# Windowed attention and a Mish MLP on one core: one third of the second product's matmuls cut into two halves of 256 columns

## The chip, the cores and the metric

The kernel runs on one core of a Trainium2 chip. The metric is the device time of one execution in microseconds: 959.55 us is the median of three runs of the kernel before (958.15 to 961.64).

## The reference

Eight batches of eight heads, 576 positions, head size 64. Each query sees itself and the 127 positions before it, with a bias that falls linearly with distance; softmax; product with V. The result, 4608 tokens of 512 values, goes through an MLP without biases:

```python
h = x @ w_in                                   # 4608x512 @ 512x2048
sp = np.where(h > 20.0, h, np.log1p(np.exp(np.minimum(h, 20.0))))
g = h * np.tanh(sp)                            # Mish
return (g @ w_out).astype(np.float32)          # 4608x2048 @ 2048x512
```

## The kernel before, in words

The tokens are cut into nine chunks of 512: the first 512 positions of each batch, and a last chunk made of the 64 left over from each. Chunk 0 is computed alone; the others go in pairs (1,2), (3,4), (5,6), (7,8).

**Numbers in two parts.** The MLP's matmuls take operands of type float32r (written `f32` in the profile's shapes, as float32 is). To keep precision every operand is held as a high part and a low part, and a product is the sum of three: high by high, high by low, low by high. For the weights W_out these parts are the tiles `so` (`w_part("o", j, 0 or 1, f)`, L180). For the Mish values ScalarE writes the high part `gh` (`parts_hi`, L433) and GpSimd subtracts to get the low part `gl` (`parts_lo`, L440); both lie in one tile `gs`, of which there are three buffers shared with others.

**The first product** of a pair of chunks (tiles `m`, `product`, L687) uses seven block products instead of eight, with weight tiles `st` streamed from DRAM. Chunk 0's is `first` (L415, tile `h`).

**The second product** is `second` (L474). One call does one chunk, one half of it (256 tokens), one of eight groups `j` of 256 hidden values, and one tile `t` of 128 tokens. It issues six matmuls into the PSUM tile `po0` or `po1`, which all accumulate over the eight `j`. In each, the stationary operand is 128x128 of the Mish values and the moving one 128x512 of W_out: two with `gh` and the high part of W_out (f = 0, 1), two with `gh` and the low part, two with `gl` and the high part. There are 9 chunks x 2 halves x 8 groups x 2 tiles = 288 calls and 1728 matmuls, each preceded by a load of its own stationary operand. `store` (L487) copies a finished `po` out on VectorE or ScalarE and sends it to DRAM.

**Attention** of the next pair runs between the calls of the second product. Its matmuls have float32 operands (tiles `s`, `o`, `pt_0l` to `pt_3l`), shorter moving operands, and come in bursts; `idle` (L131) issues bf16 matmuls of a zero tile `busy` early on, 49 in all, up to seven in a row.

**What sets the order.** All work is a list of closures with due times (`put`, L730), sorted, and issued in that order; each engine's stream keeps program order (`InOrder`, L20, from whose L30 every instruction is recorded, so the profile is read by tile names). In the last stretch (from 868 us) only the second product of the last pair is left.

Of the kernel before, what the change touches and what calls it, by code (L numbers as in the profile page):

```python
# [16 lines left out]
P = 128  # L17
# [20 lines left out]
def attention_mish_mlp(  # L38
# [19 lines left out]
    NT, DM = out.shape  # L58
    S = NT // B
    DFF = w_in.shape[0] * 256  # L60
    w_ = {"i": w_in, "o": w_out}
# [3 lines left out]
    NJ = DFF // 256  # L65
# [11 lines left out]
    pe, dve, act, pool, sp = [  # L77
        InOrder(tc, e) for e in (nc.tensor, nc.vector, nc.scalar, nc.gpsimd, nc.sync)
    ]
# [100 lines left out]
    def w_part(kind, j, part, c):  # L180
        assert (kind, j) in ready
        n = 256 if kind == "i" else DM
        return wt[(kind, j)][:, part, c * n : c * n + n]
# [264 lines left out]
    po = {}  # L448
# [25 lines left out]
    def second(c, half, j, t):  # L474
        gh, gl, _ = gs[(c, half, j)]
        if j == 0:
            po[t] = ps.tile([P, DM], F32, tag=f"po{t}", name=f"po{c}_{half}_{t}")
        k = 0
        for g, w_ in ((gh, 0), (gh, 1), (gl, 0)):
            for f in range(2):  # L480
                k += 1
                pe.matmul(
                    po[t], lhsT=g[:, f, t * P : (t + 1) * P], rhs=w_part("o", j, w_, f),
                    start=(j == 0 and k == 1), stop=(j == NJ - 1 and k == 6),
                )

    def store(c, half, t):  # L487
        ob = out_tile(c, half, t)
# [45 lines left out]
    for j in range(NJ):  # L534
        t = X0 + SLOT * j
# [189 lines left out]
    for s in range(len(PAIRS) + 1):  # L725
# [7 lines left out]
        for o, c in enumerate(chunks):  # L733
            o *= 4 * NJ
            for m in range(2 * NJ):
                for t in range(2):
                    put(o + 2 * m + t, second, c, *divmod(m, NJ), t)
                    if m % NJ == NJ - 1:
                        put(o + 2 * m + t, store, c, m // NJ, t)
                if s == 0 and m >= 2:  # L740
                    t = PARTS[m - 2]
                    put(t, parts_hi, c, *divmod(m, NJ))
                    put({3.7: 4.05, 8.9: 9.05, 19.7: 20.05}.get(t, t), parts_lo, c, *divmod(m, NJ))
                elif o + m >= 2:
                    put(o + 2 * m - 4.1, parts, c, *divmod(m, NJ))
# [11 lines left out]
        if s < len(PAIRS):  # L757
# [30 lines left out]
            for k in range(len(PROD)):  # L788
                n = 1 if s == 0 and k < 2 else 2
                for i in range(0, NF // 2, n):  # L790
# [4 lines left out]
                    for m in range((1, 2, 1, 2, 2, 3, 2)[k]):  # L795
                        t = L + 8 * k + i + n + (0, 0.6, 2.5)[m] * (1 if m else 0)
                        if s == 0 and k < 2:
                            t = (t - 0.4, L + 24.6 + 0.8 * i)[m]
                        if m == 1 and k in (3, 5):
                            t = L + 8 * k + i + n + 0.1  # L800
# [90 lines left out]
```

## Time and profile before

| | |
|---|---|
| median of three runs | 959.55 us |
| the profiled execution | 960.24 us |
| its span (first to last instruction) | 958.5 us |
| mean granted TensorE clock | 0.996 |
| TensorE matmul busy | 936.0 us (98%) |
| TensorE weight load busy | 750.6 us (78%) |
| VectorE, ScalarE, GpSimd busy | 485.2, 416.3, 374.9 us |

A matmul's recorded time contains a pipeline that overlaps the next matmul's, so its mean of 395 ns is not what it costs. The cost of one is the pitch, the distance from one start to the next, which comes out of a run's length divided by its count. PEld rows are the weight loads, which are recorded beside the matmuls.

### The profile page before, as it was taken

How to read it: one execution, taken by the hardware profiler on the slowest of the kernel's cores; microseconds unless marked ns; L12 is line 12 of the kernel's file. 1: busy time of each engine (PE TensorE's matmuls, PEld its weight loads, DVE VectorE, ACT ScalarE, POOL GpSimd, SP SyncE). 2: the span in 40 equal slices, each digit the busy share in tenths (PEclk: the TensorE clock that was granted, in tenths of full speed). 3: DMA queues.
4: the chain of work that ended last, by engine and by line, in shares of the span. 5: the costliest groups of instructions: out<-in, count | busy, mean ns of one | idle time of the engine just before them, and what ended most of it. 6: DMA issues, size and time to landing. Idle time of an engine off the chain costs nothing.

```text
span 958.5 us, 14123 instructions
## 1 busy us (share of the span) xinstructions
PE 936.0 (98%) x5133; PEld 750.6 (78%) x5137; DVE 485.2 (51%) x1280; ACT 416.3 (43%) x978; POOL 374.9 (39%) x292
## 2 busy tenths in 40 slices
PE   8998899998999999999999999999999999999998
PEld 4676677776888888888888888888888888888886
DVE  6888876684545554554555645455455105451000
ACT  5784654544455343352453534343634224243221
POOL 3201777523443434104544343014534430344443
PEclk9999999999999999999999999999999999999999
DMA  9999335787403233565221324555120144540010
GB/s 371 427 420 422 114 110 185 265 303 249 168 29 108 62 88 110 168 203 192 88 71 65 108 66 142 201 185 197 41 68 15 68 154 156 200 150 0 23 34 34
DMA packets 53286, 145.24 MB, mean 152 GB/s; under 512 B 9056, under 2 KB 10464, under 8 KB 49888
## 3 DMA queue, kind: packets, MB, share of 16 engines
q1 hardware_dynamic: 51840, 143.54, 42.6%
q8 instruction: 41, 0.67, 0.3%
q10 hardware_dynamic: 1376, 0.79, 0.3%
q14 instruction: 29, 0.24, 0.1%
HBM read 113.90 MB, written 30.41 MB: 151 GB/s over the span
## 4 chain that ended last, share of the span: by engine, by line
PE 82%; DVE 1%; DMA 1%; ACT 1%; POOL 0%; issue 0%; POOLq 0%
PE po L30 39%; PE m L30 30%; PE s L30 7%; PE o L30 5%; DMA st<-wcS 1%; PE pt_3l L30 1%; PE pt_2l L30 1%; PE pt_1l L30 1%; PE pt_0l L30 1%; ACT pz L30 0%; DVE pz L30 0%; DVE B L30 0%; POOL pz L30 0%; ACT cw L30 0%; DVE xT L30 0%
## 5 line engine op out<-in xcount | busy, mean ns | idle before, releaser
L30 PE MATMUL po<-so,gs 128*128 128x512 f32 x1728 | 411.7, 395 | 0.0
L30 PEld LDWEIGHTS po<-so,gs 128*128 128x128 f32 x1728 | 321.1, 189 | 65.8
L30 PE MATMUL m<-xT,st 128*128 128x512 f32 x768 | 177.8, 392 | 2.8 <-DMA st<-wcS 2.8
L30 PEld LDWEIGHTS m<-xT,st 128*128 128x128 f32 x768 | 145.1, 189 | 34.3 <-ACT x L30 2.3
L30 PE MATMUL m<-x,st 128*128 128x512 f32 x576 | 135.5, 392 | 1.0 <-DVE B L30 0.8
L30 POOL TENSOR_TENSOR pz<-pz,sm 128x512 f32<-128x512 f32 x64 | 66.6, 1042 | 165.9 <-DVE sm L30 67.0
L30 PEld LDWEIGHTS m<-x,st 128*128 128x128 f32 x576 | 107.1, 188 | 24.5 <-DVE B L30 0.9
L30 ACT ACTIVATE pz<-pz,mx 128x128 f32<-128x128 f32 x256 | 99.4, 390 | 43.0 <-DVE mx L30 40.6
L30 POOL TENSOR_TENSOR D<-A,C 128x1024 f32<-128x1024 f32 x16 | 38.3, 2395 | 162.7 <-DVE A L30 133.3
L30 DVE COPY ob<-po 128x512 f32<-128x512 f32 (+1 forms) x19 | 12.9, 678 | 154.3 <-PE po L30 153.2
L30 DVE TENSOR_TENSOR pz<-s,masks 128x1024 f32<-128x1024 f32 x56 | 66.3, 1216 | 35.5 <-PE s L30 32.6
L30 PE MATMUL s<-qk 64*128 64x256 f32 (+1 forms) x512 | 58.6, 365 | 3.5 <-ACT g L30 3.4
L30 DVE CUSTOM_DVE_ANT_0 pz<-s,nb 128x128 f32<-128x128 f32 x256 | 59.2, 287 | 2.8
L30 DVE TENSOR_TENSOR A<-m,A 128x1024 f32<-128x1024 f32 x32 | 39.2, 1224 | 40.3 <-PE m L30 40.3
L30 POOL TENSOR_TENSOR gs<-D,gs 128x512 fp32r<-128x512 f32 x32 | 41.1, 1288 | 43.0 <-ACT gs L30 43.0
L30 POOL TENSOR_TENSOR C<-A,C 128x1024 f32<-128x1024 f32 x16 | 38.4, 2400 | 48.7 <-DVE A L30 37.2
L30 POOL TENSOR_TENSOR gs<-B,gs 128x512 fp32r<-128x512 f32 x32 | 41.0, 1285 | 33.6 <-ACT gs L30 33.4
L30 POOL TENSOR_TENSOR gs<-A,gs 128x512 fp32r<-128x512 f32 x32 | 41.1, 1288 | 32.0 <-ACT gs L30 31.8
L30 PEld LDWEIGHTS s<-qk 64*128 64x128 f32 x512 | 41.1, 187 | 12.1 <-ACT g L30 3.8
L30 POOL TENSOR_TENSOR gs<-C,gs 128x512 fp32r<-128x512 f32 x32 | 40.9, 1286 | 23.0 <-ACT gs L30 23.0
L30 PE MATMUL o<-pz,va 128*64 128x128 f32 (+1 forms) x560 | 48.7, 320 | 0.0
L30 DVE COPY_PREDICATED s<-older,s 128x256 f32<-128x256 uint16 x64 | 35.8, 559 | 24.7 <-PE s L30 24.7
(155 smaller groups left out, 1051.4 us busy)
## 6 DMA issues: line engine op xcount, KB each, us to landing
st<-wcS SPq DMA_DIRECT2D x64, 512.0 KB, 4.6
st<-wr SPq DMA_DIRECT2D x48, 512.0 KB, 5.5
qk<-in_qk_dram SPq DMA_DIRECT2D x31, 640.0 KB, 4.9
va<-in_v_dram SPq DMA_DIRECT2D x28, 320.0 KB, 3.3
wi<-in_moe_w_in_dram SPq DMA_DIRECT2D x8, 1024.0 KB, 14.5
wo<-in_moe_w_out_dram SPq DMA_DIRECT2D x8, 1024.0 KB, 19.7
wr<-si SPq DMA_DIRECT2D x8, 1024.0 KB, 13.1
wcS<-cw SPq DMA_DIRECT2D x16, 512.0 KB, 5.8
```

The lines of the kernel that those rows point to most:

```text
L30: ins = method(*args, **kwargs)
```

## The change

In `second` the two matmuls with `gl` (the fifth and sixth of a call, `k > 4`) are each issued as two, over columns 0 to 255 and 256 to 511 of W_out and of `po`, with the same stationary operand. The other four are as before. Every matmul of the call gets `skip_group_check=True`, an argument of the program's builder, not of the instruction. No load, wait, buffer or due time is changed.

```diff
         for g, w_ in ((gh, 0), (gh, 1), (gl, 0)):
             for f in range(2):
                 k += 1
-                pe.matmul(
-                    po[t], lhsT=g[:, f, t * P : (t + 1) * P], rhs=w_part("o", j, w_, f),
-                    start=(j == 0 and k == 1), stop=(j == NJ - 1 and k == 6),
-                )
+                for d in range(2 if k > 4 else 1):
+                    n = slice(256 * d, 256 * d + 256) if k > 4 else slice(0, DM)
+                    pe.matmul(
+                        po[t][:, n], lhsT=g[:, f, t * P : (t + 1) * P], rhs=w_part("o", j, w_, f)[:, n],
+                        start=(j == 0 and k == 1), stop=(j == NJ - 1 and k == 6), skip_group_check=True,
+                    )
```

## Rows read from the trace of the kernel before

**Rows 1.** The page, its head and parts 1 and 4: busy time of the engines, and the chain of waits by engine and by line (share of the span).

```profile
span 958.5 us, 14123 instructions
PE 936.0 (98%) x5133; PEld 750.6 (78%) x5137; DVE 485.2 (51%) x1280; ACT 416.3 (43%) x978; POOL 374.9 (39%) x292
PE 82%; DVE 1%; DMA 1%; ACT 1%; POOL 0%; issue 0%; POOLq 0%
```

**Rows 2.** The chain of waits in order of time, pieces of tile `po` (the second product): start in us, length in us, what, number of instructions.

```profile
480.45 8.26 PE po L30 x36
489.70 2.78 PE po L30 x12
496.69 8.26 PE po L30 x36
...
749.35 42.41 PE po L30 x186
...
867.92 87.05 PE po L30 x384
```

**Rows 3.** Groups of instructions by tile and shape, TensorE's matmuls and its weight loads: count, busy us, mean ns of one, idle us before.

```profile
L30 PE MATMUL po<-so,gs 128*128 128x512 f32 x1728 | 411.7, 395 | 0.0
...
L30 PE MATMUL idle<-busy 128*128 128x512 bf16 x45 | 13.7, 419 | 1.5 <-DVE busy L30 1.3
...
L30 PEld LDWEIGHTS po<-so,gs 128*128 128x128 f32 x1728 | 321.1, 189 | 65.8
...
L30 PEld LDWEIGHTS <-busy 128*128 128x128 bf16 x49 | 4.8, 103 | 5.8 <-issue 1.7 <-DVE busy L30 1.3
```

**Rows 4.** Busy time by stretch of the span: us, then per engine busy us (instructions), then granted clock, share of the DMA engines, GB/s. The first is the early stretch of Rows 7, the second the last stretch of the kernel.

```profile
96.50:99.40 2.90, 2.90 (x9) 2.25 (x9) 2.87 (x10) 1.33 (x3) 1.72 (x1) 0.53 1.01 362
868.00:954.90 86.90, 86.90 (x384) 71.68 (x382) 3.99 (x5) 21.25 (x34) 38.63 (x30) 1.00 0.07 19
```

**Rows 5.** The timeline of TensorE's weight loads around 480 us: start, length, engine, what, count.

```profile
479.79 0.52 PEld L30 LDWEIGHTS pt_0l<-qk 128*128 128x128 f32 x4 [0.33 <-issue]
480.23 2.84 PEld L30 LDWEIGHTS po<-so,gs 128*128 128x128 f32 x13
```

**Rows 6.** The timeline of TensorE's matmuls: eight float32 transposes of attention and what follows them; and two runs of bf16 matmuls of 512 columns early on.

```profile
602.19 1.03 PE L30 MATMUL s<-ident,pz 128*128 128x128 f32 x8
603.06 0.27 PE L30 MATMUL pt_3l<-ident,pz_3l 128*128 128x128 f32 x1
...
6.94 1.47 PE L30 MATMUL idle<-busy 128*128 128x512 bf16 x6
...
10.11 1.03 PE L30 MATMUL idle<-busy 128*128 128x512 bf16 x4
```

**Rows 7.** Second-product matmuls at the lower clock: the timeline from 96.46 us, and the tile's durations (ns, min/median/max) with first and last start.

```profile
96.46 3.17 PE L30 MATMUL po<-so,gs 128*128 128x512 f32 x7
...
L30 PE MATMUL po<-so,gs x1728: 387/389/628, 89.1 to 954.6; 128*128 128x512 f32 x192
```

**Rows 8.** Waits of TensorE, the longest: who waited for whom, us in total, times, longest us.

```profile
PE s L30 <- POOL pz L30: 5.4, 5, 1.9
PE s L30 <- ACT g L30: 3.4, 1, 3.4
PE m L30 <- DMA st<-wcS: 2.8, 3, 2.0
```

**Rows 9.** The waits of other engines for the second product, and the page's row of the queue that brings instructions.

```profile
DVE ob L30 <- PE po L30: 153.2, 18, 21.1
ACT gs L30 <- PE po L30: 131.8, 88, 3.1
...
q8 instruction: 41, 0.67, 0.3%
```

## The prediction

> **What bounds the kernel now.** I read the page's busy times and chain first: TensorE is busy for 936.0 of 958.5 us and holds 82% of the chain, every other engine 1% or less [rows 1]. So a nanosecond more or less on TensorE's stream is nearly a nanosecond of the kernel, and the question is only what the stream costs. Then the chain in order of time, because it shows long unbroken runs of the second product: 384 matmuls in 87.05 us and 186 in 42.41 us, a pitch of 226.7 and 228.0 ns (the first start of the 186 follows a burst of attention); beside attention a run of 36 takes 8.26 us (229.4 ns each) and a run of 12 takes 2.78 us (231.7 ns) [rows 2]. The reader is to see two things. The second product is limited by TensorE's own rhythm: in the last stretch matmuls fill 86.90 of 86.90 us at full granted clock, with DMA at 0.07 and VectorE, ScalarE and GpSimd busy for 4.0, 21.3 and 38.6 us [rows 4]. And that rhythm depends on what ran before: the runs that start after attention's short matmuls lose 60 ns (12 x 5.0) or 100 ns (36 x 2.7), so a run of 512-column matmuls is slow for about its first ten and then settles at 226.7.
>
> **The price of one 256-column matmul.** None of the kernel's float32r matmuls has fewer than 512 columns, so it is bounded from rows beside it. At one column per cycle of 2.4 GHz 512 columns stream for 213.3 ns, and the settled pitch holds 13.4 ns more; 256 columns stream for 106.7.
>
> *Floor.* Each matmul brings its own weight load: 1728 for 1728 in the second product, and the 49 matmuls of the zero tile, up to seven in a row with one stationary operand, have 49 loads too [rows 3]. So the second half of a pair reloads what the first had; the change adds 576 matmuls and 576 loads. Loads of 128x128 float32, of attention and then of the second product, follow each other in (480.23 - 479.79)/4 = 110 ns when nothing longer lies between them [rows 5], though each is recorded with 189 ns [rows 3]. Transposes, of 128 columns, go at (603.06 - 602.19)/8 = 109 ns [rows 6]. A pair can hardly take less than 2 x 110 = 220 ns.
>
> *Ceiling.* If the 13.4 ns are a fixed surcharge of each matmul or each load, a half costs 106.7 + 13.4 = 120.1 and a pair 240.
>
> *Between.* If they are a part of the streaming, a half costs 113.3 and a pair what one matmul cost. For this speaks the stretch at half clock (granted 0.53 in its mean, [rows 4]): seven second-product matmuls in 3.17 us, of which the last lasts 0.63, so (3.17 - 0.63)/6 = 423 ns [rows 7], with 512 columns at 1.2 GHz worth 426.7. That is one column per cycle, and no surcharge is left where the stream is slower. And the bf16 matmuls of 512 columns have a pitch of (1.47 - 1.03)/2 = 220 ns [rows 6], nearer to the bare 213, with a load each as well.
>
> I take the streaming view, a surcharge that goes with the columns, since a fixed one should be seen at half clock too; both ends stay in the range.
>
> **The change, part by part.** Per call four matmuls of 512 stay and two become four halves.
>
> 1. *Rhythm.* Now two runs go almost wholly at the settled pitch, 570 matmuls in 87.05 + 42.41 us, 227.1 each; the other 1158 lie beside attention, 48 of them in 8.26 + 2.78 = 11.04 us, or 230.0 each [rows 2]. The mean is (570 x 227.1 + 1158 x 230.0)/1728 = 229.0 ns. With the change the widths alternate every four matmuls, so there is never a run of ten equal ones in which the pitch could settle. The nearest row for that is the run of 12, 231.7 ns per 512 columns [rows 2], and I take it for whole matmuls and for a pair of halves (115.9 each, over the loads' 110) alike: 1728 x (231.7 - 229.0) = **+4.7 us**.
> 2. *Accumulation, PSUM, waits.* The halves write disjoint halves of the same bank in the same order. The waits on ScalarE, GpSimd and VectorE have no new member: nobody waits on the first half, and the last half signals as the last matmul did. Zero.
> 3. *Other engines.* They wait for the second product, not it for them (ScalarE 131.8 us for `gs` buffers, VectorE 153.2 us for finished `po` [rows 9]); a later release finds idle engines. Zero, unless the stream got so much faster that GpSimd, busy for 38.6 of 86.9 us in the last stretch, came due; that is far off.
> 4. *Instructions.* 1152 more on 14123, at 0.3% of the DMA engines for the queue that brings them [rows 1, 9]. Zero: the queue's share would grow by a twelfth of 0.3%, and the DMA engines are at 0.07 in the last stretch [rows 4].
> 5. *What could swallow some.* TensorE waits 2.8 us for streamed weights, 5.4 us for GpSimd, 3.4 us for ScalarE [rows 8]. Those waits lie early, beside chunk 0, which has 32 of the 288 calls; at most a ninth of the addition, 0.5 us, is hidden there. I count none.
>
> Sum: 960.24 (the profiled execution: 958.5 of span and 1.7 around it) + 4.7 = 964.9. The median of the runs is 0.7 below the profiled execution, so 964.2 us.
>
> **A rule that would make it worse.** In the run of 384 the weight loads are busy for 71.7 of the 86.9 us in which matmuls are busy without a gap [rows 4], and the pitch of 226.7 is far under a stream and a load laid end to end, 213.3 + 110. The Trainium skill ("TensorE: Matmul & The Clock Gate", Part 3, under "What overlaps and what doesn't") says that a weight load overlaps a running matmul only when it uses another row group. By that rule these full-height loads would stand between the matmuls, which the trace contradicts at 512 columns; what it would make of 256 is the last of the rivals.
>
> **The rivals.**
>
> *Nothing measurable.* The rhythm settles in the mixed sequence as well and a half costs 112 to 115: against 229.0 a pair brings -5.0 to +1.0 ns, times 576 -2.9 to +0.6 us: 956.7 to 960.1. For it: the half-clock rows, and that the long runs settle in any event. Against it: each change of width in the trace is followed by a slow stretch.
>
> *Faster.* The halves run at the loads' 110 and the whole ones settle at 226.7: a call is 4 x 226.7 + 4 x 110 = 1346.8 against 6 x 229.0 = 1374.0, 27.2 x 288 = -7.8 us at the very most; with the unsettled starts after attention kept, (220 - 229.0) x 576 = -5.2 us: 954.4. It decides once a half takes less than 112 ns. To it belongs the case that the builder drops the second load of a pair, against which the 49 loads of the idle matmuls speak.
>
> Its neighbour by a page: the Trainium skill (same page, "Back-to-back issue gap") gives N/2.4 + 2.5 ns for a warm matmul, 109 for 256 columns, an estimate that would put a pair near 218 and the kernel a little under the faster case; the trace's 226.7 at 512 columns is above its 216.
>
> *Fixed surcharge.* A half costs 120.1: (240.2 - 229.0) x 576 = +6.5 us: 966.0. With the rhythm lost on the 1152 whole ones too (2.7 each, 3.1 us): 969.1.
>
> *The load stands bare.* A 256-column stream is too short to cover a load, and the full 110 comes on top of each added matmul: 576 x 110 = +63 us: 1023. It decides if a load's recorded 189 ns, not its spacing, has to pass before the next matmul. Against it: the transposes' 109 [rows 6].
>
> **How the numbers follow.** A measurement of this kernel can tell about 0.3% (2.9 us) from no change. Chances: rhythm lost 0.36 (its size runs from 2 to 8 us, so a third of it lies within 0.3%); nothing measurable 0.29; fixed surcharge, with or without the rhythm, 0.20; faster 0.11; bare load 0.04. Slower: 0.24 + 0.20 + 0.04 = 0.48; within 0.3%: 0.12 + 0.29 = 0.41; faster 0.11. The range goes from 956 to 971: it holds the first three with their bounds and leaves out the bare load and the faster case's deeper part. The likeliest case's own range is 961 to 967.
>
> **What would show it.** In the profile after: 2304 matmuls and 2304 loads on `po`, 1152 of them 128x256. In the last run (now 87.05 us) 512 matmuls in 64 calls; rhythm lost gives 64 x 1390 = 89.0 us, proportional 87.1, fixed surcharge 88.8 with whole ones still at 226.7, faster 86.2. The starts tell the first from the third: whole matmuls at 230 or more, or at 226.7 with halves at 120. The gain or loss must appear evenly per call, in every stretch with second-product work; `m` runs stay as they are. I am wrong if the halves' pitch is under 112 or over 121, if the loads show gaps in front of matmuls that aren't there now, or if the time moves elsewhere than in `po`.

## The result and the profile after

The changed kernel takes 965.37 us in the median (965.24 to 966.25), 5.8 us more than the 959.55 of before: ratio 1.0069, 95% interval 1.0054 to 1.0084 (ratios here and below are the record's, not quotients of the medians). One execution of a kernel below, the whole bf16 matmuls, took 1330.64 us at a mean granted clock of 0.655 and is in no median. The 965.37 is inside the forecast's range and close to its 964.2, but the sum got there with two errors that nearly cancel, as the experiments show.

The page's head, and TensorE's groups by shape (count, busy us, mean ns of one, idle before), answer to [rows 1, 3]:

```profile
span 963.7 us, 15273 instructions
PE 943.2 (98%) x5709; PEld 784.4 (81%) x5713; DVE 485.3 (50%) x1280; ACT 416.6 (43%) x978; POOL 375.3 (39%) x292
...
L30 PE MATMUL po<-so,gs 128*128 128x512 f32 x1152 | 319.7, 399 | 0.0
L30 PE MATMUL po<-so,gs 128*128 128x256 f32 x1152 | 182.8, 280 | 0.0
...
L30 PEld LDWEIGHTS po<-so,gs 128*128 128x128 f32 x2304 | 358.1, 189 | 51.1
```

Each half has its own weight load, 2304 for 2304, so the change did add 576 loads. VectorE, ScalarE and GpSimd do what they did. The chain in order of time answers to [rows 2]:

```profile
479.33 8.45 PE po L30 x48
488.76 2.77 PE po L30 x16
...
750.39 43.70 PE po L30 x248
794.08 76.21 PE m L30 x336
870.29 89.80 PE po L30 x512
```

The last run has grown from 87.05 to 89.80 us, the one from 750 from 42.41 to 43.70, the first product between them is the same 76.2 us. A call now takes 89.80/64 = 1403 ns against 1360. Beside attention eight calls take 8.45 + 2.77 = 11.22 us against 11.04. There are 20 such units up to 750 us, worth 20 x 0.18 = 3.6 us, but at 749 to 750 us the two profiles were only 1.04 us apart: some 2.6 us came back before 274 us, where the first of these units starts. Starts of the halves and wholes of one call, from the timeline (start, length, what; the count is of what overlaps a moment):

```profile
890.68 0.52 PE L30 MATMUL po<-so,gs 128*128 128x256 f32 x3
...
891.15 0.63 PE L30 MATMUL po<-so,gs 128*128 128x512 f32 x2
...
892.09 0.40 PE L30 MATMUL po<-so,gs 128*128 128x256 f32 x2
```

Four halves begin at 890.68, four whole matmuls at 891.15, the next halves at 892.09: 119 ns a half and 232 a whole one by the unrounded starts (890.678, 891.155, 892.085). Over the last stretch the starts give means of 118.5 and 232.2: 4 x 118.5 + 4 x 232.2 = 1403.

### The profile page after: what moved, and what is told of

Same layout as the page of the kernel before. It is cut to its first block, busy times and chain, and to the rows that moved or that the text cites. A ratio compares the mean times of both kernels' runs of the same rounds, so it can differ in the third digit from the quotient of the medians.

```text
span 963.7 us, 15273 instructions
## 1 busy us (share of the span) xinstructions
PE 943.2 (98%) x5709; PEld 784.4 (81%) x5713; DVE 485.3 (50%) x1280; ACT 416.6 (43%) x978; POOL 375.3 (39%) x292
## 4 chain that ended last, share of the span: by engine, by line
PE 83%; DVE 1%; ACT 1%; DMA 1%; issue 0%; POOL 0%; SPq 0%; POOLq 0%
PE po L30 40%; PE m L30 30%; PE s L30 7%; PE o L30 5%; PE pt_3l L30 1%; DMA st<-wcS 1%; PE pt_2l L30 1%; PE pt_1l L30 1%; PE pt_0l L30 1%; ACT pz L30 0%; DVE B L30 0%; POOL pz L30 0%; ACT cw L30 0%; DVE cw L30 0%; DVE pz L30 0%
## 5 line engine op out<-in xcount | busy, mean ns | idle before, releaser
L30 PE MATMUL po<-so,gs 128*128 128x256 f32 (+1 forms) x2304 | 419.5, 340 | 0.0
L30 PEld LDWEIGHTS po<-so,gs 128*128 128x128 f32 x2304 | 358.1, 189 | 51.1
```

Of the source, the lines that this page charges most:

```text
L30: ins = method(*args, **kwargs)
```

## The experiments

Three questions: is the price of a half a share of the streaming or fixed per matmul, and whose is it; is the lost rhythm real; and where did 2.6 us come back? `A` and `B` in the expectations are the forecast and its rival, the fixed surcharge.

**All matmuls as halves.**

```diff
-                for d in range(2 if k > 4 else 1):
-                    n = slice(256 * d, 256 * d + 256) if k > 4 else slice(0, DM)
+                for d in range(2):
+                    n = slice(256 * d, 256 * d + 256)
...
-    start=(j == 0 and k == 1)
+    start=(j == 0 and k == 1 and d == 0)
```

> All six matmuls of a call are issued as two halves, so the second product is one even stream of 256-column matmuls. Theory A (the surcharge goes with the columns, and only the alternation of widths unsettles the pitch): the even stream settles, halves at about 113.3 ns, the last stretch at 768 x 113.3 = 87.0 us as before the change, the kernel within 2 us of the one before. Theory B (each matmul carries a fixed surcharge of some 12 to 13 ns, whatever its width): halves at 118 to 120, the last stretch at 91 to 92 us, the kernel (237 to 240 - 229) x 1728 = 14 to 19 us above the one before. If only the loads bounded it: 110 to 112 each, 85 us.

Measured 976.66 us against 959.61 (ratio 1.0173, 1.0156 to 1.0190), +17.1. The last run in the chain:

```profile
879.06 92.16 PE po L30 x768
```

92.16/768 = 120.0 ns, and single starts are 120 apart throughout: 106.7 of streaming and 13.3 more, the very surcharge of a settled 512-column matmul. So in an even stream it is the same for 256 columns as for 512, fixed per matmul or per load. The streaming share (113.3) is out.

**Halves in one group of eight.**

```diff
-                for d in range(2 if k > 4 else 1):
+                for d in range(2 if k > 4 and j == 0 else 1):
...
```

The column slice gets the same condition, here and in the next two kernels.

> The halves are issued only for j = 0, so in the last stretch two calls of halves in a row (t = 0, 1) stand before 14 calls of whole matmuls, 84 in a row. Theory A (alternation unsettles): whole matmuls behind the halves run at 229 to 236 for about ten, then at 226.7 up to the next halves; the last stretch is 87.05 + 4 x (2 calls' worth of lost rhythm, 0.05 to 0.1 us each) = 87.3 to 87.5 us; the kernel within 1 us of the one before. Theory B (fixed surcharge, no rhythm): whole matmuls stay at 226.7 all through, halves 118 to 120.

Measured 960.26 against 959.61 us (1.0004, 0.9994 to 1.0013). The timeline behind the second group of halves, at three whole matmuls:

```profile
892.45 0.63 PE L30 MATMUL po<-so,gs 128*128 128x512 f32 x2
...
894.31 0.62 PE L30 MATMUL po<-so,gs 128*128 128x512 f32 x2
...
896.35 0.62 PE L30 MATMUL po<-so,gs 128*128 128x512 f32 x2
```

The eight matmuls from 892.45 to 894.31 take 232 ns each, the nine from there to 896.35 take 227. The rhythm is lost after a change of width and found again after about nine, as the forecast had it; in the changed kernel the next change comes after four.

**Chunk 0 without, and chunk 0 alone.**

```diff
-                for d in range(2 if k > 4 else 1):
+                for d in range(2 if k > 4 and c else 1):        # one kernel
+                for d in range(2 if k > 4 and c == 0 else 1):   # the other
...
```

> The halves are issued in all chunks but chunk 0. After the change the stages from 267 us on had grown by 7.7 us together, while the part before, with chunk 0, had shrunk by 2.6. If that shrinking comes from chunk 0's halves, it is gone here: the kernel is 7 to 8 us above the one before. If it is scatter of one execution, the kernel is 5 to 6 us above the one before, as with all chunks, less chunk 0's own 0.5.

> The halves are issued in chunk 0 alone (32 of 288 calls). If chunk 0's halves shorten the early part: 2 to 3 us below the kernel before. If not: 0 to 1 us above it.

Measured 967.53 (1.0076, 1.0060 to 1.0092) and 957.97 (0.9983, 0.9972 to 0.9993) against 959.61 us: +7.9 and -1.6, together the change's +5.8 within their intervals. The same edit costs 7.9/256 = 0.031 us per call in eight chunks and gains in the first.

**Columns cut at 384.**

```diff
-                    n = slice(256 * d, 256 * d + 256) if k > 4 else slice(0, DM)
+                    n = slice(384 * d, 384 + 128 * d) if k > 4 else slice(0, DM)
```

> The low product's matmuls are cut at column 384, not 256. If a half's 120 ns (the even stream of halves) is a surcharge of 13.3 ns on the streaming of any float32r matmul, the 384 columns take 160.0 + 13.3 = 173 ns and the 128 columns what the weight load behind them lets through, 110 to 112 (their own stream would be 67): a pair at 285, 26 to 28 us above the kernel before. If 120 is instead the spacing of the loads, the 128 columns take 120 too, a pair 293, 31 us above. If the surcharge goes with the columns, 384 take 170 and 128 110: a pair at 280, 24 us above.

Measured 990.66 against 959.15 us (1.0335, 1.0320 to 1.0350), +31.5: above the totals expected for a surcharge, which were worked out against the changed kernel's pair of 237 ns and not the 229 of before. From the last start of the first pair's `m` (270 us) to the end the kernel grew by 31.2 us over 256 calls, 122 ns a call: 2 x (284 - 229) for the pairs, as the pieces below give, and 3 for each of the four whole matmuls, which lose the rhythm here too. What the same 122 ns make of chunk 0's 32 calls, 3.9 us, has come back before that but for 0.3. The weight loads give the spacing of the pieces (a short matmul's recorded start lies ahead of its load's end):

```profile
897.09 0.30 PEld L30 LDWEIGHTS po<-so,gs 128*128 128x128 f32 x2
...
897.19 0.19 PEld L30 LDWEIGHTS po<-so,gs 128*128 128x128 f32 x1
...
897.37 0.30 PEld L30 LDWEIGHTS po<-so,gs 128*128 128x128 f32 x2
...
897.48 0.19 PEld L30 LDWEIGHTS po<-so,gs 128*128 128x128 f32 x1
```

The 384 columns take 0.18 us (172 to 179 ns: 160 and some 13 to 19), the 128 columns 0.11 us (109 ns), the spacing of loads. So loads can follow every 109 ns, and 120 is not their spacing: the surcharge is on top.

**Short loads.** The low product's stationary operand has 64 columns; half its tokens get no low product.

```diff
+                m = P if k < 5 else 64
                 pe.matmul(
-                    po[t], lhsT=g[:, f, t * P : (t + 1) * P], ...
+                    po[t][:m], lhsT=g[:, f, t * P : t * P + m], ...
...
```

> No halves; the low product's two matmuls keep 512 columns but have a stationary operand of 64 columns, so that their weight loads are half as long (the other 64 tokens of each 128 get no low product: left out). The loads run beside the fourth and fifth matmul of a call. Theory L (the surcharge is what the next load takes from the running stream): the fourth and fifth drop to about 220, the kernel about 288 x 2 x 6.7 = 4 us below the one before. Theory M (the surcharge belongs to the float32r matmul): all stay at 226.7 in the last stretch and the kernel is within 1 us of the one before.

Measured 961.50 against 959.15 us (1.0032, 1.0020 to 1.0044). Neither theory has this: the pitch went up in the long runs (the runs of 12 beside attention stayed at 2.76 us).

```profile
867.90 88.32 PE po L30 x384
```

88.32/384 = 230.0 ns, with starts 224 to 236 apart and no settling. A load of half the columns (recorded with 134 ns for 188) gained nothing: the fourth and fifth matmul of a call, beside which it runs, average 228 and 229 ns and not the 220 of theory L. But a change of the stationary operand's columns (of the matmul and its load alike) disturbs the rhythm as a change of width does.

**A bf16 matmul in place of the low product,** on a zero tile, in halves and whole (the low product is left out). The halves' edit:

```diff
+    zero = const.tile([P, 512], BF16, tag="zero", name="zero")
+    dve.memset(zero, 0.0)
...
-                        po[t][:, n], lhsT=g[:, f, t * P : (t + 1) * P], rhs=w_part("o", j, w_, f)[:, n],
+                        po[t][:, n], lhsT=zero[:, :P] if k > 4 else g[:, f, t * P : (t + 1) * P],
+                        rhs=zero[:, n] if k > 4 else w_part("o", j, w_, f)[:, n],
```

> As after the change, but the low product's four halves are bf16 matmuls of a zero tile (the low product is left out). Theory M: a bf16 half takes 109 ns and no surcharge, only the last one waits for a float32r load (110 to 113); whole matmuls between them are unsettled at 232: a call at 4 x 232 + 4 x 110 = 1368, the last stretch at 87.5 us, the kernel 1 to 2 us below the one before. Theory L: the last half, beside which a float32r load runs, takes 120, the whole matmul ahead of the first half, beside which a bf16 load runs, drops to about 216.

> The low product as two bf16 matmuls of 512 columns on a zero tile (the low product is left out). Theory M: these two take 216 ns each; the four others 226.7 if the rhythm of equal widths is kept, 232 if any change of kind unsettles it: a call at 1339 or 1360 against 1374, the kernel 10 or 4 us below the one before. Theory L: the fourth matmul drops too, the sixth does not: the same sum, other places.

Measured 960.91 (1.0020, 1.0010 to 1.0029) and 960.72 us (1.0019, 1.0009 to 1.0029) against 959.15. The halves' kernel, timeline of weight loads, then of matmuls:

```profile
897.30 0.33 PEld L30 LDWEIGHTS <-zero 128*128 128x128 bf16 x4 [0.27 <-issue]
897.65 0.76 PEld L30 LDWEIGHTS po<-so,gs 128*128 128x128 f32 x4
898.68 0.33 PEld L30 LDWEIGHTS <-zero 128*128 128x128 bf16 x4 [0.27 <-issue]
```

```profile
897.31 0.61 PE L30 MATMUL po<-zero 128*128 128x256 bf16 x4
897.67 1.17 PE L30 MATMUL po<-so,gs 128*128 128x512 f32 x4
898.69 0.50 PE L30 MATMUL po<-zero 128*128 128x256 bf16 x3
```

The starts of the bf16 halves are 120 (the first, whose load has not been done beforehand), 109 and 110 apart, and the fourth takes 110 too, though a float32r load runs beside it. But 109 is also the spacing of loads, so halves alone cannot show what a bf16 matmul carries. Whole ones can: the loads of the other kernel, and 14 in a row out of the next experiment:

```profile
897.90 0.12 PEld L30 LDWEIGHTS <-zero 128*128 128x128 bf16 x2 [0.27 <-issue]
898.13 0.87 PEld L30 LDWEIGHTS po<-so,gs 128*128 128x128 f32 x4
...
898.35 0.19 PEld L30 LDWEIGHTS po<-so,gs 128*128 128x128 f32 x1
```

```profile
90.42 3.19 PE L30 MATMUL fill<-zero 128*128 128x512 bf16 x14
```

The second whole bf16 matmul takes 216 ns, from the float32r load that starts with it (898.13) to the next (898.35), and the row of 14, of which the last lasts 0.38, has (3.19 - 0.38)/13 = 216. So bf16 carries 2.7 ns on 213.3, and a float32r load beside it costs nothing. The float32r matmul ahead of the bf16 ones takes 230 to 232 with no load beside it at all (the loads idle for 0.27 us). Both speak against theory L: the 13.3 ns go with the float32r matmul (theory M) or with the change to its own weights, which no run separates. The bf16 operands are zeros, so type and values are not separated either.

The expected gain of the bf16 kernels is missing all the same. With halves a call takes 898.69 - 897.31 = 1.38 us against 1360 ns before: the four halves take 449 ns, and the four whole ones 233 each. With whole ones the chain's last stretch goes

```profile
869.43 12.23 PE po L30 x53
...
881.73 12.23 PE po L30 x53
```

nine calls in 12.30 us, 1367 ns a call: two bf16 matmuls at 222 in their mean are cheaper, but the first pays for its load, and the four float32r ones between changes of kind run at 231.

**Fills in the early waits.** For the 2.6 us the suspect is TensorE's clock. In the kernel before TensorE waits 2.0 us for streamed weights at 223 us (start to start 2.3), and in the stretch from 222 to 232 us the granted clock is 0.83; in the changed kernel the wait there is 1.1 us (1.5) and the clock stays at 1.00.

```diff
+    def fill(n):
+        t = ps.tile([P, 512], F32, tag="po1", name="fill")
+        for _ in range(n):
+            pe.matmul(t, lhsT=zero[:, :P], rhs=zero, start=True, stop=True)
...
+                put(0.79, fill, 14)
+                put(L + 19.999, fill, 6)
```

> No halves; bf16 matmuls of a zero tile are put into two early waits of TensorE: 14 (3.0 us) into the wait of 3.8 us at 91 us, 6 (1.3 us) into the wait of 2.3 us at 223 us. In the kernel before each of these waits is followed by a stretch of 3.4 us at half clock. Theory C (the early difference of executions is the clock: each such stretch costs 1.7 us): both stretches go, the kernel is 1.5 to 3.5 us below the one before. Theory D (the clock falls anyway, or the waits are longer by what is saved): within 0.5 us of the one before.

> The same fills, and the halves in chunk 0 alone. With halves in chunk 0 alone and no fill the kernel was 1.6 us below the one before. If that gain came from a half-clock stretch at 223 us that the later arrival avoids, the fills already hold it, and this kernel is 0 to 1 us above the one with fills and no halves. If it has another source (fewer waits for GpSimd), it stays: 1.5 us below the one with fills.

> The kernel before, unchanged, for a second profiled execution. If the stretch at half clock near 226 us belongs to the kernel, it is there again; if it is scatter, the span is 1.7 us nearer to 956.8, and the m stage from 174 us ends 1.7 us earlier after its start than the 96.5 us of the first profile.

Measured: 958.52 (0.9990, 0.9982 to 0.9999) with fills, 957.98 (0.9982, 0.9974 to 0.9991) with fills and halves in chunk 0, against 960.08 us; a single 961.57 for the kernel before. Busy time from 222 to 232 us (columns as in [rows 4]) of the kernel before once more, then with fills, then of chunk 0's halves alone:

```profile
222.00:232.00 10.00, 7.99 (x28) 6.11 (x27) 2.30 (x3) 8.03 (x13) 0.00 (x0) 0.83 0.89 342
```

```profile
222.00:232.00 10.00, 8.32 (x37) 6.63 (x36) 2.52 (x3) 8.32 (x13) 1.26 (x1) 1.00 0.88 330
```

```profile
222.00:232.00 10.00, 9.11 (x41) 7.26 (x40) 2.93 (x4) 7.99 (x12) 1.69 (x1) 1.00 0.93 341
```

Both profiles of the kernel before show half clock there (0.83 is the mean of the ten microseconds; single matmuls start 427 ns apart), after a wait of 2.0 us without matmuls; 28 matmuls fit into the ten microseconds, 37 with the fills, 41 with chunk 0's halves. But the second fill did not go into that wait. First the kernel before, then with fills:

```profile
225.09 2.24 PE L30 MATMUL m<-xT,st 128*128 128x512 f32 x7 [1.95 <-DMA st<-wcS]
```

```profile
217.65 1.47 PE L30 MATMUL fill<-zero 128*128 128x512 bf16 x6
...
226.29 0.93 PE L30 MATMUL m<-xT,st 128*128 128x512 f32 x3 [1.68 <-ACT x L30]
```

The six ran at 217.65 us, and a wait of 1.68 us stayed (start to start 2.1). Full clock also came after waits of 1.9 us (halves in all chunks but chunk 0) and 2.1 us (short loads). So the wait's length alone does not decide, and how a fill keeps the clock is not shown. What half clock costs is. From the first to the last start of the first pair's `m`, in the 13 profiles:

| first to last start of `m`, us | clock, 222 to 232 us | kernels |
|---|---|---|
| 96.3 to 96.5 | 0.83 | before (both profiles), bf16 whole |
| 94.3 to 94.7 | 1.00 | one group in eight, all chunks but chunk 0, short loads, fills |
| 93.8 to 94.1 | 1.00 | the six with all of chunk 0's low product in pieces, the changed kernel among them |

Half clock costs this stage some 1.9 us, as 0.83 over ten microseconds should (1.7), and chunk 0's halves save some 0.6 more: TensorE's waits from 210 to 232 us are 2.8 us in the kernel before and 2.0 in the changed one. The stage took 93.8 us in the changed kernel and 96.5 in the profile before, which is the 2.6 us but for a start 0.2 us later. So most of them are the clock.

Half clock there comes and goes. The 67 executions of the kernel before beside these experiments lie in three steps, 23 at 957.8 to 958.9 us, 37 at 959.1 to 961.1, 7 at 961.4 to 962.3; of chunk 0's halves alone nine of twelve lie at 957.6 to 958.3 and three at 959.4 to 959.6. The shortest executions are equal (957.77 and 957.61); with chunk 0's halves they are commoner. The mean clock of an execution does not tell them apart (seven of the nine have the 0.996 of the middle step): it does not say where the half clock fell. The profile of chunk 0's halves is one of the three longer executions; from 112 to 122 us it has a clock of 0.83, as the second profile of the kernel before has and the first has not (1.00), and its `m` starts at 175.5 us, theirs at 175.1 and 173.6.

The fills bring 1.6 us in the median, as chunk 0's halves do; both together bring 0.5 more, which these intervals don't separate from nothing. The fill at 91 us kept the clock there too (86 to 100 us: 1.00 against 0.88), but gained nothing there: TensorE came earlier and waited for GpSimd instead.

```profile
103.86 0.66 PE L30 MATMUL s<-ident,pz 128*128 128x128 f32 x4 [1.46 <-POOL pz L30]
```

```profile
103.73 0.66 PE L30 MATMUL s<-ident,pz 128*128 128x128 f32 x4 [3.04 <-POOL pz L30]
```

The first row is of the kernel before, the second with fills: the wait grew from 1.46 to 3.04 us.

## Why the prediction was right, and where it was not

*What bounds the kernel:* as forecast. TensorE's stream got longer and the kernel with it, by what the chain's runs of `po` show: 20 x 0.18 + 1.29 + 2.75 = 7.6 us, call by call in every stage from 270 us on, where the profiles grew by 7.7.

*Floor:* right. No load was dropped, and loads every 109 ns never bound a half.

*Between (the price of a half):* wrong, and the step that failed. I took the surcharge for a part of the streaming because it is gone at half clock; the even stream of halves shows 13.3 ns on 256 columns as on 512. A surcharge can be hidden at half clock and still be fixed at full clock. The other support, the bf16 pitch, said nothing of float32r: bf16 carries 2.7 ns. A pair costs 237.0 in the changed kernel instead of the 231.7 of the sum: (237.0 - 231.7) x 576 = 3.1 us too little.

*Rhythm:* right in kind and size: whole matmuls at 232.2 against 231.7 forecast, shown by the group of eight. The two together are the rival that I priced at 969.1 (fixed surcharge with the rhythm lost). Without chunk 0's halves the kernel is at 967.5 with eight ninths of the calls. So the likeliest case had half of the mechanism, and its 964.2 was luck.

*Point 5 (what could swallow some):* wrong by its size and sign. I counted nothing for chunk 0, at most 0.5 us hidden. Chunk 0's own addition, some 0.9 us, is hidden, the later arrival shortens TensorE's waits, and none of the six profiles with it has half clock behind them: -1.6 us in the median for chunk 0's halves alone. This and the half's price nearly cancel, which is why 964.2 came so near to 965.4.

*Steps 2 to 4:* zero, as forecast. VectorE, ScalarE and GpSimd are busy for the same time; ScalarE waits longer for `gs` buffers (160.9 against 131.8 us), which costs nothing, since the runs of `po` go on without a gap. The instruction queue's 45 packets for 41 don't show.

*Bare load:* out, by the 109 ns of the 128-column pieces. The Trainium skill's rule that a load overlaps a matmul only in another row group ("TensorE: Matmul & The Clock Gate", Part 3) is contradicted again: full-height loads run beside full-height float32r matmuls at every width tried. Only where the kind changes from float32r to bf16 did a load stay behind. The Trainium skill's N/2.4 + 2.5 ns for a warm matmul (same page, "Back-to-back issue gap") holds here for bf16 (216 ns at 512 columns) and not for float32r (226.7; 120.0 at 256).

What stays open: why a float32r matmul carries 13.3 ns at full clock, why its pitch takes about nine matmuls to settle, and what decides whether half clock follows a wait near 223 us. The runs show how large the surcharge is, what disturbs the pitch and what half clock costs, not what is behind them.

## What to carry to other kernels

Price a cut in a matmul's moving columns from an even stream of the narrower ones in the same type, and read settled and unsettled pitch apart: a uniform run and a short run behind a change give two prices. Mixing widths, load sizes or types in one stream of float32r matmuls costs the neighbours too, here 5.5 ns on each of four; a cheaper matmul in the middle can lose its whole gain that way. And before adding or removing work ahead of a wait of TensorE, look at the granted clock behind it, in more than one profile and beside the spread of the executions: a little delay can be worth more than it costs.

## What the runs showed of the hardware that was not expected

- A float32r matmul of full height costs its columns at 2.4 GHz and 13.3 ns more, 120.0 ns for 256 and 226.7 for 512, in an even stream with a load for each; bf16, zeros with a load for each, takes 216 for 512.
- After a change of width, of the stationary operand's columns (128 to 64), or of type, the pitch of 512-column float32r matmuls wanders between 224 and 236 ns and settles only in a run of equal ones (about nine); with stationary operands of two sizes in turn it never settled in 384 matmuls (230.0 ns).
- At a change from float32r to bf16 the bf16 load was not done ahead: the loads idle for 0.27 us and the first bf16 half takes 120 ns instead of 109.
- Half clock followed waits of 1.8 to 2.0 us of TensorE in three profiles, and did not follow waits of 1.7 to 2.1 us at the same place in four others.
